# Linear attention and a routed expert layer on one core: the expert stage ordered without the rule that kept VectorE's two-operand instructions apart from GpSimd's gathers and scatters

## The chip, the cores and the metric

The kernel runs on one core of a Trainium2 chip. The metric is the device time of one execution in microseconds; lower is better. All times are of that one core.

## The reference

Two layers in a row. The first is a linear attention over 8 batches, 8 heads, 576 positions and 64 channels: queries and keys are projected to 128 features, shifted by their largest absolute value, and taken through exp(x) and exp(-x); the rows of the result, 4608 tokens of 512 numbers, go to the second layer. That is a layer of 8 experts with capacity: every token goes to one expert, every expert takes 576 tokens, and the pairs of token and expert are given out in the order of their logits.

```python
logits = x @ w_gate                       # 4608 x 8
order = np.argsort(-logits.flatten())
for idx in order:                         # greedy, cap = 576 tokens an expert
    tok, e = (int(idx) // E, int(idx) % E)
    if assigned[tok] >= 0 or counts[e] >= cap:
        continue
    assigned[tok] = e
    counts[e] += 1
for e in range(E):
    mask = assigned == e
    h = np.maximum(x[mask] @ w1[e], 0.0)  # 512 -> 1024
    out[mask] = h @ w2[e]                 # 1024 -> 512
```

## The kernel before, in words

The attention comes first (to about 310 us of the profile) and writes the token rows `xs` to HBM and the logits `L` to SBUF. The change does not touch it.

The greedy assignment is done expert by expert: of the experts still open, the one that fills first at the highest threshold gives up its 576 tokens, those are taken out of `L`, and the next is looked for. I number the experts 0 to 7 in the order in which they run. The routing of one expert (`routing`, lines 512 to 660) is a long chain of small steps between VectorE and TensorE: the key of each token's best logit is cut into six digits, and for each digit VectorE compares (L532), TensorE counts (L542 or L546), VectorE folds (L548, L550), TensorE sums (L553), VectorE makes a flag (L558), TensorE spreads it (L560), and VectorE picks the digit and goes on (L562, L566). Then ranks and indices are made (L584 to L648; the last matmul of that is L642, the index tile is `idx`), and the taken tokens are masked (L652 to L660, the step called `up`). The routing of expert r + 1 runs in the shadow of expert r's matmuls. Only expert 0's routing stands alone.

One expert's work: GpSimd gathers its 576 rows of `xs` with five indirect DMAs into `xg` (L751, the steps `ga`). TensorE transposes them in three sets (the steps `xp`: two sets of 16 matmuls at L771, one of 4 at L757; expert 0 has five sets of 4 at L757), ScalarE copies each into the rounded part `xh` (L758, L776), VectorE makes the remainder `xl` (L759, L777). The weights come through SP's queue as `raww` (L673), ScalarE rounds them (L735), VectorE makes the remainders `w1l` and `w2l` (L738, L739). The first layer is 16 products of 12 matmuls each (L797: rounded times rounded, and the two cross terms; 8 column blocks times two token halves of 272 and 304), each followed by a ReLU on ScalarE (L808, L809: `fh`, `ff`) and its remainder on VectorE (L812: `fl`). The second layer has five token blocks: four of 24 matmuls (L826, the steps `y`, planned in pairs) and one of 32 small ones (L841). ScalarE copies a block out of PSUM (L849, `ysb`), and GpSimd scatters it to the output with an indirect DMA (L855, the steps `ys`), after a small memset (L854).

What sets the order of all this is a planner, the class `Plan` (lines 18 to 90). Every step is put in with `add`: an engine, a planned duration, a due time, the steps it depends on, buffers it takes and frees, and a flag `lock`. `order` places them one after the other, always the step that can start earliest on its engine by the planned times, due times deciding. The result is fixed when the kernel is built: each engine's instructions stand in the order of the planned start times, and on the chip each engine takes them in that order and waits on semaphores for what isn't ready. The planned times themselves do nothing on the chip.

The flag `lock` has two sides in `order`, both for the plan alone (`self.dl` is the planned end of the last locked step of VectorE):

```python
if x['lock'] and e=='DVE': s=max(s,free.get('POOL',0.))
if x['lock'] and e=='POOL': s=max(s,self.dl)
```

A locked step of VectorE is planned to start when GpSimd is free; a locked step of GpSimd when the last locked step of VectorE has ended. In the expert stage the routing steps, the weight remainders, the gathers and the scatters have it.

Buffers that matter: one `xg`, one pair `xh`/`xl`, three `idx`, four PSUM buffers `h` shared by first-layer products and transposes, two `y`, two `ysb`.

## Time and profile before

| what | value |
|---|---|
| three runs | 808.28, 808.34 and 811.11 us, median 808.34 |
| the profiled execution | 810.09 us |
| its span, first to last instruction | 808.3 us |
| mean granted clock of TensorE | 0.975 |
| busy: TensorE | 770.2 us, 95% |
| busy: VectorE | 549.5 us, 68% |
| busy: ScalarE | 360.0 us, 45% |
| busy: GpSimd | 262.4 us, 32% |
| HBM read, written | 71.40 MB, 18.87 MB |

A row of the profile's groups reads: line, engine, operation, output<-inputs, shape, count | busy us, mean ns of one | idle time of the engine just before them, and what ended it. A row of the timeline reads: start us, length us, engine, line, operation, count [idle before <- what ended it]. PEld is TensorE's weight load, which overlaps its matmuls.

### The profile page before, as it was taken

To read this page: it belongs to the slowest core of one execution; us is meant where nothing else is said; L and a number is where in the kernel's file an instruction comes from. 1 tells how busy PE (TensorE), PEld (TensorE's weight loads), DVE (VectorE), ACT (ScalarE), POOL (GpSimd) and SP (SyncE) were. 2 spreads that over 40 slices of the span, in tenths; PEclk is the share of its full clock that TensorE was granted. 3 is DMA by queue.
4 is the path that set the end of the run, shared out by engine and by line. 5 is a ranking of instruction groups with operands and counts; after the bars stand their busy time and mean duration, and the time that the engine had idled before them with its cause. 6 is when DMAs were issued, how large, how long until landed. Compare 5 with 4: busy or idle time off the path is not lost.

```text
span 808.3 us, 23640 instructions
## 1 busy us (share of the span) xinstructions
PE 770.2 (95%) x10047; PEld 663.4 (82%) x10047; DVE 549.5 (68%) x1494; ACT 360.0 (45%) x625; POOL 262.4 (32%) x299
## 2 busy tenths in 40 slices
PE   6899999999999995599999999999999999999995
PEld 4788888888888885498798798798797897897983
DVE  5877888788788866787597486686585585550410
ACT  2866777676767750233343243233243233441410
POOL 3865555566665550300401302203103104302011
PEclk9999999999999996589999999999999999999998
DMA  8844454454444111532424415405323333801300
GB/s 181 178 120 120 135 147 135 127 150 134 128 120 119 33 37 56 163 105 82 158 88 133 130 66 157 155 18 187 137 63 128 137 100 116 273 2 41 124 27 32
DMA packets 73516, 91.80 MB, mean 114 GB/s; under 512 B 5155, under 2 KB 56515, under 8 KB 73411
## 3 DMA queue, kind: packets, MB, share of 16 engines
q1 hardware_dynamic: 67040, 71.06, 29.8%
q0 software_dynamic: 5952, 18.91, 7.1%
q8 instruction: 79, 1.29, 0.7%
q10 hardware_dynamic: 418, 0.33, 0.2%
q14 instruction: 27, 0.21, 0.1%
HBM read 71.40 MB, written 18.87 MB: 112 GB/s over the span
## 4 chain that ended last, share of the span: by engine, by line
PE 44%; issue 12%; POOL 2%; DVE 1%; DMA 0%; POOLq 0%; ACT 0%; DVEq 0%
PE h L797 20%; PE y L826 17%; PE y L841 2%; PE rps L546 1%; POOL out_dram L855 1%; PE rps L542 1%; PE h L771 1%; POOL xg L751 1%; PE h L757 1%; DMA xg<-xs,idx 0%; PE rps L623 0%; PE rps L560 0%; DVE cmp L618 0%; DVE cc L566 0%; POOLq L919 0%
## 5 line engine op out<-in xcount | busy, mean ns | idle before, releaser
L797 PE MATMUL h<-xh,w1h 128*128 128x272 f32 (+1 forms) x512 | 146.6, 307 | 0.7 <-ACT xh L758 0.7
L797 PE MATMUL h<-xh,w1l 128*128 128x272 f32 (+1 forms) x512 | 143.1, 299 | 0.0
L855 POOL DMA_INDIRECT out_dram<-ysb,idx x40 | 41.4, 1035 | 210.7 <-ACT ysb L849 201.0
L808 ACT ACTIVATE fh<-h 128x272 fp32r<-128x272 f32 (+1 forms) x128 | 49.3, 385 | 132.4 <-PE h L797 111.8
L826 PE MATMUL y<-w2h,fl 128*128 128x512 f32 x256 | 101.7, 397 | 0.0
L826 PE MATMUL y<-w2l,fh 128*128 128x512 f32 x256 | 101.1, 395 | 0.0
L826 PE MATMUL y<-w2h,fh 128*128 128x512 f32 x256 | 101.0, 394 | 0.0
L797 PEld LDWEIGHTS h<-xh,w1h 128*128 128x128 f32 x512 | 97.3, 190 | 2.0 <-ACT xh L758 1.1
L797 PEld LDWEIGHTS h<-xh,w1l 128*128 128x128 f32 x512 | 97.6, 191 | 0.0
L751 POOL DMA_INDIRECT xg<-xs,idx x40 | 40.5, 1012 | 172.6 <-issue 135.7
L797 PE MATMUL h<-xl,w1h 128*128 128x272 f32 (+1 forms) x512 | 91.4, 297 | 0.0
L270 ACT ACTIVATE qP<-D 128x768 f32<-128x768 f32 x96 | 72.8, 814 | 40.8 <-PE D L132 40.7
L812 DVE SCALAR_TENSOR_TENSOR fl<-h,fh 128x272 fp32r<-128x272 f32 (+1 forms) x128 | 52.6, 419 | 53.4 <-ACT fh L808 41.2
L211 POOL TENSOR_TENSOR ks<-ks,kP 128x512 f32<-128x512 f32 x64 | 81.6, 1278 | 4.6
L287 PE MATMUL D<-kz,qP 128*64 128x73 f32 x2304 | 79.9, 227 | 0.0
L287 PEld LDWEIGHTS D<-kz,qP 128*64 128x64 f32 x2304 | 75.4, 136 | 2.3
L210 POOL TENSOR_TENSOR ks<-kP 128x512 f32<-128x512 f32 x32 | 40.7, 1272 | 111.3 <-issue 87.2
L849 ACT COPY ysb<-y 128x512 f32<-128x512 f32 (+1 forms) x40 | 21.8, 545 | 122.4 <-PE y L826 58.8
L797 PEld LDWEIGHTS h<-xl,w1h 128*128 128x128 f32 x512 | 75.5, 188 | 0.0
L164 DVE TENSOR_REDUCE km<-D 128x6 f32<-128x768 f32 x48 | 45.7, 954 | 27.3 <-PE D L160 26.8
L198 PE MATMUL D<-kP,vi 128*64 128x256 f32 x512 | 61.8, 382 | 0.4 <-ACT kh L174 0.4
L164 DVE TENSOR_REDUCE qm<-D 128x6 f32<-128x768 f32 x48 | 45.5, 952 | 17.3 <-PE D L160 17.2
(179 smaller groups left out, 1461.7 us busy)
## 6 DMA issues: line engine op xcount, KB each, us to landing
raww<-in_moe_w_dram SPq DMA_DIRECT2D x64, 512.0 KB, 5.3
qi<-in_q_dram SPq DMA_DIRECT2D x32, 288.0 KB, 5.0
xs<-xp SPq DMA_DIRECT2D x16, 576.0 KB, 4.5
ki<-in_k_dram SPq DMA_DIRECT2D x32, 160.0 KB, 4.1
vi<-in_v_dram SPq DMA_DIRECT2D x32, 160.0 KB, 3.1
vi<-in_v_dram SPq DMA_DIRECT2D x32, 128.0 KB, 3.1
ki<-in_k_dram SPq DMA_DIRECT2D x30, 128.0 KB, 3.7
xg<-xs,idx POOLq DMA_INDIRECT x40, 3.5
```

The lines of the kernel that those rows point to most:

```text
L164: V.tensor_reduce(m[:,:,0:n],X['v'],axis=AX.X,op=OP.max,apply_absolute_value=True)
L198: PE.matmul(kv[64*c:64*c+64,i,0:256],v_[:,a,s_,:],kP[:,b,:],start=b in (0,5,9,14),stop=False,skip_group_check=True)
L210: if i==0: G.tensor_add(ks[:,:,a],X(0),X(1))
L211: elif i<3: G.tensor_add(ks[:,:,a],ks[:,:,a],X(i+1))
L270: for fh in range(2): A.activation(rows(qP[:,fh]),halves(X['T'],6),AF.Exp,scale=1.0-2*fh)
L287: PE.matmul(p[64*ab:64*ab+64,c,m:m+73],T['qP',u,jj][:,fh,o,64*ab:64*ab+64],T['kz',u][:,ab,fh,a^ab,:],start=fh==0,stop=fh==1,skip_group_che ...
L751: G.indirect_dma_start(out=T['xg',r][0:n,bb,:],out_offset=None,in_=xs,in_offset=bass.IndirectOffsetOnAxis(ap=T['idx',r][0:n,bb,:],axis=0))
L797: PE.matmul(p,ws[:,k,o:o+128],xx[:,k,o1:o2],start=n==0,stop=n==11)
L808: A.activation(hh[:,f,o1:o1+m1],p[:,0:m1],AF.Relu)
L812: V.scalar_tensor_tensor(hl[:,f,o1:o1+m1],p[:,0:m1],0.0,hh[:,f,o1:o1+m1],op0=OP.max,op1=OP.subtract)
L826: PE.matmul(p,hx[:,f,o:o+128],ws[:,f%2,:],start=n==0,stop=n==23)
L855: st=G.indirect_dma_start(out=ov,out_offset=bass.IndirectOffsetOnAxis(ap=iv,axis=0),in_=yv,in_offset=None)
```

## The change

Four lines of `moe` change. The flag `lock` goes from three steps: `up` of expert 0 on VectorE, every gather and every scatter on GpSimd. In the plan, GpSimd's gathers and scatters then no longer wait for VectorE's locked steps. VectorE's other locked steps (routing, weight remainders) keep the flag, and so still wait for GpSimd in the plan. The planned time of expert 0's transposes goes from 109 to 90 ns each. The long lines are the calls of `add` themselves.

```diff
--- before.py
+++ after.py
@@ -696,7 +696,7 @@
         return z
     def up0(x):
         for _ in it0: pass
-    add(('up',0),'DVE',1750.,2.,up0,lock=True)
+    add(('up',0),'DVE',1750.,2.,up0)
     prev=('up',0)
     for r in range(1,E):
         it=routing(r)
@@ -749,7 +749,7 @@
             def ga(y,r=r,bb=bb,n=n):
                 if bb==0: T['xg',r]=fp.tile([128,5,Dm],F32,name='xg',bufs=1)
                 G.indirect_dma_start(out=T['xg',r][0:n,bb,:],out_offset=None,in_=xs,in_offset=bass.IndirectOffsetOnAxis(ap=T['idx',r][0:n,bb,:],axis=0))
-            add(('ga',r,bb),'POOL',1250.,b+d['g']+.1*bb if r else bb*.1,ga,[('idx',r)] if r else [],slot=(('xg',1,('xg',r)),) if bb==0 else (),frees=(('idx',r),) if r else (),lat=2600.,lock=True,seq=('ga',r,bb-1) if bb else None)
+            add(('ga',r,bb),'POOL',1250.,b+d['g']+.1*bb if r else bb*.1,ga,[('idx',r)] if r else [],slot=(('xg',1,('xg',r)),) if bb==0 else (),frees=(('idx',r),) if r else (),lat=2600.,seq=('ga',r,bb-1) if bb else None)
             if r and bb<4: continue
             def xp_(y,r=r,bb=bb,o=o,n=n):
                 if bb==0: tokens(r)
@@ -758,7 +758,7 @@
             def xhf(y,r=r,bb=bb,o=o,n=n): A.copy(T['xt',r][0][:,:,o:o+n],T['xp',r,bb][:,:,0:n])
             def xlf(y,r=r,bb=bb,o=o,n=n): V.tensor_sub(T['xt',r][1][:,:,o:o+n],T['xp',r,bb][:,:,0:n],T['xt',r][0][:,:,o:o+n])
             due=b-d['TE']+d['xt']+2.8 if r else bb*.5
-            add(('xp',r,bb),'PE',4*(109. if n==128 else 62.),due,xp_,[('ga',r,bb)],seq=('xp',r,bb-1 if r==0 else 2) if bb else None,mode='A' if n==128 else 'H',slot=(('h',4,('xp',r,bb)),)+((('xt',1,('xt',r)),) if bb==0 else ()),frees=(('xg',r),))
+            add(('xp',r,bb),'PE',4*(90. if n==128 else 62.),due,xp_,[('ga',r,bb)],seq=('xp',r,bb-1 if r==0 else 2) if bb else None,mode='A' if n==128 else 'H',slot=(('h',4,('xp',r,bb)),)+((('xt',1,('xt',r)),) if bb==0 else ()),frees=(('xg',r),))
             add(('xh',r,bb),'ACT',70+.83*4*n,due+.5,xhf,[('xp',r,bb)])
             add(('xl',r,bb),'DVE',DV(4*n),due+1.,xlf,[('xh',r,bb)],frees=(('xp',r,bb),))
         for bb in (0,2) if r else ():
@@ -857,7 +857,7 @@
                 SC.append(st)
             due+=5.5 if nn==128 else 3.5
             add(('yc',r,bb),'ACT',480. if nn==128 else 280.,due+d['y'],yc,[lastq],slot=(('ysb',2,('ysb',r,bb)),),frees=(('y',r,bb),))
-            add(('ys',r,bb),'POOL',1250.,due+d['y']+.5,ys,[('yc',r,bb)],frees=(('ysb',r,bb),)+((('idx',r),) if r else ()),lat=2800.,lock=True)
+            add(('ys',r,bb),'POOL',1250.,due+d['y']+.5,ys,[('yc',r,bb)],frees=(('ysb',r,bb),)+((('idx',r),) if r else ()),lat=2800.)
     for i in range(cfg.get('warm',0)):
         if i%16==0: p=ps.tile([128,512],F32,name='h%d'%(i//16),bufs=1)
         PE.matmul(p[:,0:128],ones,ones,start=True,stop=True)
```

The program has the same instructions; what moves is their order, on every engine. Three places follow.

GpSimd, the gathers for expert 2 (tile `xg_7742` before, `xg_7725` now) among the scatters of expert 1's blocks (`ysb`). Before:

```order
L751 DMA xg_7742<-xs_57,idx_7708 128x512
L854 MEMSET spacer_776 1x1
L855 DMA out_0_dram<-ysb_7738,idx_6933 4608x512
L751 DMA xg_7742<-xs_57,idx_7708 128x512
L854 MEMSET spacer_776 1x1
L855 DMA out_0_dram<-ysb_7789,idx_6933 4608x512
L751 DMA xg_7742<-xs_57,idx_7708 128x512 x2
L854 MEMSET spacer_776 1x1
L855 DMA out_0_dram<-ysb_7862,idx_6933 4608x512
L751 DMA xg_7742<-xs_57,idx_7708 64x512
```

Now:

```order
L751 DMA xg_7725<-xs_57,idx_7696 128x512 x3
L854 MEMSET spacer_776 1x1
L855 DMA out_0_dram<-ysb_7753,idx_6933 4608x512
L751 DMA xg_7725<-xs_57,idx_7696 128x512
L751 DMA xg_7725<-xs_57,idx_7696 64x512
```

Before, scatters of three blocks stood between the five gathers; now one does. For experts 3, 4, 5 and 6 none does.

TensorE, the first transposes for expert 4 in expert 3's second layer; `y_9341` before is the PSUM tile of that layer's block 1, `y_9312` now that of its block 0. Before, the first set stands behind the whole of block 1:

```order
L826 MATMUL y_9341<-w2l_8972,fh 128x512
L826 MATMUL y_9341<-w2h_8971,fh 128x512
L826 MATMUL y_9341<-w2h_8971,fl 128x512
L826 MATMUL y_9341<-w2l_8972,fh 128x512
L771 MATMUL h_9390<-ident,xg 128x64
```

Now it stands behind the 14th matmul of block 0:

```order
L826 MATMUL y_9312<-w2h_8968,fl 128x512
L826 MATMUL y_9312<-w2l_8969,fh 128x512
L826 MATMUL y_9312<-w2h_8994,fh 128x512
L826 MATMUL y_9312<-w2h_8994,fl 128x512
L771 MATMUL h_9353<-ident,xg 128x64
```

The transposes come 34 second-layer matmuls earlier in the stream, and the routing of expert 5 that follows them moves ahead with them. So it is, by 10 to 34 matmuls, for experts 1 to 6.

TensorE, the start of the expert stage, expert 0's transposes (L757) and first products (L797). Before:

```order
L757 MATMUL h_6309<-ident,xg 128x128 x4
L797 MATMUL h_6320<-xh,w1h_6261 128x272
L797 MATMUL h_6320<-xh,w1l_6262 128x272
L797 MATMUL h_6320<-xh,w1h_6261 128x272
L757 MATMUL h_6334<-ident,xg 128x128 x4
```

Now:

```order
L757 MATMUL h_6309<-ident,xg 128x128 x4
L757 MATMUL h_6320<-ident,xg 128x128 x4
L797 MATMUL h_6325<-xh,w1h_6261 128x272
L797 MATMUL h_6325<-xh,w1l_6262 128x272
L797 MATMUL h_6325<-xh,w1h_6261 128x272
```

The fourth set of transposes has changed places with three matmuls. On ScalarE, the second of the token copies (L758) now stands ahead of the weight cast (L735) that stood ahead of it.

## The prediction

> **What bounds the kernel now.** I read first the page's slices of time, then the stretches of single experts, then who waited for whom, then the chain that ended last. The slices put the TensorE row beside its granted clock:
>
> ```profile
> PE   6899999999999995599999999999999999999995
> ...
> PEclk9999999999999996589999999999999999999998
> ```
>
> There are two holes only: the routing of expert 0 (slices 16 and 17, about 310 to 340 us, where the clock falls as well), and the end. I call the experts 0 to 7 in the order in which they run. The expert stage is everything behind the hole. In the table of stretches (length, then busy us and count of PE, PEld, DVE, ACT, POOL, then granted clock) one expert's period reads
>
> ```profile
> 404.00:462.00 58.00, 58.00 (x465) 50.46 (x466) 42.17 (x134) 20.40 (x43) 10.59 (x15) 1.00 0.33 104
> ```
>
> TensorE is busy 58.00 of 58.00 us at full clock, VectorE 42.17 and GpSimd 10.59. A busy TensorE is modelled, so I look at who waited between 404 and 809 us. Asked for TensorE's matmuls alone the list is empty; GpSimd's gathers are the ones that sit still, and nothing that the profile shows ends it:
>
> ```profile
> POOL xg L751 <- issue: 130.5, 29, 32.0
> ```
>
> The groups by form show the idle time ahead of the matmuls in the last column, and it is zero:
>
> ```profile
> L826 PE MATMUL y<-w2h,fl 128*128 128x512 f32 x224 | 89.1, 398 | 0.0
> L797 PE MATMUL h<-xh,w1h 128*128 128x304 f32 x224 | 66.2, 311 | 0.0
> ```
>
> The chain that ended last gives the true spacing of the stream (start, length, what, count):
>
> ```profile
> 438.71 11.00 PE y L826 x48
> 449.71 0.65 PE h L771 x16
> 450.36 4.77 PE y L826 x20
> ...
> 487.97 3.27 PE h L797 x24
> ```
>
> That is 0.229 us a second-layer matmul, 0.458 for the pair that the planner moves as one step, 0.136 us a first-layer matmul, 0.65 for a set of 16 transposes, and no gap between them. The stage is a packed matmul stream. Edits of order can't take matmuls out of it; they can only open waits in it, or shorten the hole ahead of it. A measurement of this kernel can tell about 0.5% (4 us) from no change.
>
> **The change part by part.** No instruction is added or removed. Three locks and one planned duration go from the planner, so it no longer holds a gather or a scatter back until VectorE's planned two-operand work ends, and no longer holds back the step that ends expert 0's routing. VectorE's own locked steps still wait, in the plan, for GpSimd. The outcome is an order.
>
> *The start.* Expert 0's fourth set of transposes now stands ahead of the first three matmuls; on ScalarE the second token copy stands ahead of a weight cast that used to precede it. The rows of this place, from the timeline, the tile xg (time to landing, between 320 and 350 us) and the stretches:
>
> ```profile
> 338.89 0.95 POOL L751 DMA_INDIRECT xg<-xs,idx  x1 [0.30 <-issue]
> 339.69 1.05 ACT L735 CAST w1h<-raww 128x1024 fp32r<-128x1024 f32 x1
> 341.27 0.59 ACT L758 CAST xh<-h 128x512 fp32r<-128x512 f32 x1 [0.53 <-PE h L757]
> 343.00 0.60 PE L797 MATMUL h<-xh,w1h 128*128 128x272 f32 x1 [0.68 <-ACT xh L758]
> 343.84 1.06 PE L757 MATMUL h<-ident,xg 128*128 128x128 f32 x4
> 344.55 0.58 PE L797 MATMUL h<-xh,w1l 128*128 128x272 f32 x1
> ...
> DMA to landing us min/median/max: 3.2/3.8/4.5
> ...
> 344.00:346.00 2.00, 2.00 (x11) 2.00 (x10) 2.00 (x6) 0.59 (x1) 0.00 (x0) 0.50 0.04 8
> 346.00:348.00 2.00, 2.00 (x19) 1.73 (x18) 1.97 (x6) 0.14 (x1) 0.00 (x0) 0.50 0.00 0
> ```
>
> The fourth gather lands at 338.89 + 3.8 = 342.7, while TensorE is idle, so its transposes fill a hole instead of taking 344.55 - 343.84 = 0.7 us of the stream. But the third copy now comes behind the cast: 341.27 + 0.59 + 1.05 + 0.59 = 343.5 instead of 343.0, so 0.5 to 0.6 is given back. Net about -0.2 us. The bounds: 0, if a step of expert 1's routing ends last here anyway; and -2.2, if the fuller stream also brought the full clock back at 344 instead of past 348 (4 us at 0.50 are worth 2 us). I take -0.2, since what TensorE does between 342 and 345 hardly gets denser.
>
> *Gathers against transposes, experts 1 to 4.* Before, the transposes of the next expert's tokens stood late in the second layer. Now the planner believes the gathers to be back to back and puts them as early as it thinks the rows arrive: the first set for expert 2 moves from the end of block 2 to the middle of block 1. Whether the rows are there is to be worked out from the step that makes the indices (the matmul of L642). Expert 2 in the trace:
>
> ```profile
> 438.53 0.18 PE L642 MATMUL rps<-d,dup 128*128 128x18 bf16 x1
> ...
> 440.08 1.13 POOL L751 DMA_INDIRECT xg<-xs,idx  x1 [34.47 <-PE y L826]
> 441.21 0.09 POOL L854 MEMSET spacer<- 1x1 f32 x1
> 441.51 0.99 POOL L855 DMA_INDIRECT out_dram<-ysb,idx  x1 [0.21 <-ACT w1h L735]
> ...
> 447.41 0.98 POOL L751 DMA_INDIRECT xg<-xs,idx  x1 [0.30 <-issue]
> 448.70 0.96 POOL L751 DMA_INDIRECT xg<-xs,idx  x1 [0.30 <-issue]
> ...
> DMA to landing us min/median/max: 2.8/3.4/3.6
> ```
>
> The first gather starts 1.55 us behind L642, the second 1.13 + 0.30 = 1.43 later, each further one 1.28 (0.98 + 0.30), and a landing takes 3.4. Now three gathers stand ahead of the first scatter. The second lands at 1.55 + 1.43 + 3.4 = 6.4; TensorE gets to the first set behind 15 pairs, at 15 x 0.458 = 6.9: no wait, 0.5 to spare (before: 449.7 against a landing by about 446). The fourth gather waits for a scatter, which waits for a block that ends at 8 pairs = 3.7 and its copy: scatter at about 5.5, fourth gather at 6.8, landed at 10.2; TensorE is there at 6.9 + 0.65 + 6 x 0.458 = 10.3. The fifth lands at 6.8 + 1.28 + 3.4 = 11.5, TensorE comes at 10.3 + 0.65 + 0.46 = 11.4. So expert 2 waits 0.1 us, or 0.5 if a copy comes late. Expert 4 is the tightest:
>
> ```profile
> 551.53 0.18 PE L642 MATMUL rps<-d,dup 128*128 128x18 bf16 x1
> ...
> 553.59 1.12 POOL L751 DMA_INDIRECT xg<-xs,idx  x1 [31.24 <-issue]
> ```
>
> Its gathers start 2.06 behind L642; all five now go in a row, the fourth at 2.06 + 1.43 + 2 x 1.28 = 6.05, landed at 9.45. TensorE has 30 first-layer matmuls (4.1), 7 pairs (3.2), a set (0.65) and 3 pairs (1.4) ahead of the second set: 9.35. That is 0.1 late, the fifth gather another 0.1; one more relu remainder ahead of the index step on VectorE may add 0.4 to each: 0.2 to 0.9, and I take 0.3. Expert 3 has the same form and I give it 0.2; expert 1, whose routing order is unchanged and which keeps about 0.5 to spare, gets none. Experts 5 to 7 gather long before, their transposes being held by the token buffer. Sum +0.6, bounds 0 and 3 x 0.9 = 2.7.
>
> *Routing of expert 7 inside expert 5.* There VectorE now has, between the index comparison and the step that TensorE's L642 waits for, two relu remainders, two weight remainders and the masking pair, and then the token remainder that frees the buffer for the last transposes:
>
> ```profile
> L812 DVE SCALAR_TENSOR_TENSOR fl<-h,fh 128x272 fp32r<-128x272 f32 x56 | 24.4, 436 | 40.3 <-ACT fh L808 40.2
> L738 DVE TENSOR_TENSOR w1l<-raww,w1h 128x512 fp32r<-128x512 f32 x53 | 35.3, 684 | 1.2 <-ACT w1h L735 1.1
> L637 DVE TENSOR_TENSOR pm<-rps,msk 128x36 f32<-128x36 f32 x6 | 1.2, 197 | 6.0 <-PE rps L623 6.0
> ```
>
> 2 x 0.44 + 2 x 0.68 + 2 x 0.20 = 2.6 us. TensorE in the same time has the 18 counting matmuls (0.46), a set (0.65) and a pair (0.46) = 1.6. If it reached the count just as the comparison ends it would wait 1.0; if VectorE is a microsecond ahead, nothing. I take +0.4.
>
> The sum: -0.2 + 0.6 + 0.4 = +0.8 us. The profiled execution took 810.09 us, its span 808.3 and 1.8 around it, so it would take 810.9. The median of the runs shown, 808.34, is 1.75 below the profiled one; the forecast for it is 808.34 + 0.8 = 809.1 us.
>
> **The rivals.** *No new waits at all.* The planned gather is longer than the measured one, so everything may be there in time; then only the start counts: -0.2, at most -2.2, thus 806.1 to 808.1. For it speaks that no row of before names a wait of TensorE, although its order was made by the same greedy rule.
>
> *Gathers held by VectorE, with no rule to keep them apart* (slower). The longest gather of before ran under a chain of weight remainders:
>
> ```profile
> 689.12 2.48 DVE L738 TENSOR_TENSOR w1l<-raww,w1h 128x512 fp32r<-128x512 f32 x4
> ...
> 690.96 1.49 POOL L751 DMA_INDIRECT xg<-xs,idx  x1 [0.30 <-issue]
> ...
> L751 POOL DMA_INDIRECT xg<-xs,idx x10: 903/970/1485, 668.1 to 698.2; - x10
> ```
>
> 1.49 against a median of 0.97 is 0.5 us. Were each of five gathers held so, the last would come 2.5 late, and experts 2, 3 and 4, which have no reserve, would wait 2.5 each, expert 1 2.0: +9.5, so 818. It decides from about 0.2 us a gather on. Against it: in before, gathers overlapped such work in plenty (440.08 took 1.13), since the lock held in the plan alone. The Trainium skill, "SBUF — State Buffer", section "Who interferes with whom", has this rival as a rule: a VectorE instruction with two SBUF inputs contends with a GpSimd instruction that reads SBUF, and whichever comes second is blocked for the whole of the first. By that rule the removed locks were worth up to a weight remainder per gather; the 1.49 agrees with some holding, the median does not agree with a full one.
>
> *The routing chain gets tight* (slower). A digit's step on VectorE in the second layer, with one weight remainder between, is
>
> ```profile
> L562 DVE TENSOR_REDUCE ch<-rps 128x1 f32<-128x8 f32 x30 | 5.0, 165 | 11.4 <-PE rps L560 10.9
> L566 DVE SCALAR_TENSOR_TENSOR cc<-cc,ch,dg 128x36 bf16<-128x36 bf16 x20 | 5.1, 256 | 0.7
> L532 DVE TENSOR_TENSOR cmp<-cc,kt 128x1152 bf16<-128x1152 bf16 x35 | 25.5, 753 | 0.3
> ```
>
> 0.17 + 0.26 + 0.68 + 0.75 = 1.9 us and about 0.2 for the product's end, against 5 pairs = 2.3 us. One more weight remainder late and TensorE waits 0.3; at three digits of five experts that is +4.5, and 813.
>
> **How the numbers follow.** Forecast (few short waits) 0.60, no new waits 0.25, gathers held 0.06, tight chain 0.09. Faster by over 0.5% needs 4 us out of a stream without gaps: 0.02, from the far end of the clock bound. Slower: the two last rivals but for their mild half, and the tail of the forecast's bounds: 0.12. The rest, 0.86, is the same. The range takes in the no-wait case down to -1.3 (it leaves out the last 0.9 of the clock bound), and upward the bounds 2.7 + 1.0 and one microsecond of the tight chain: 807.0 to 813.0.
>
> **What would show it.** Right: the same packed periods, TensorE's idle time in waits for xg no more than a microsecond in all, gathers of experts 2 to 4 in rows of three to five, transposes right behind their landing, ScalarE's third copy at 343.5. Wrong: transposes that wait over a microsecond for xg (gathers held if L751 grows past 1.1 us on average), waits of L546, L553 or L560 for VectorE (tight chain), or an expert period under 57 us, which nothing here explains.

## The result and the profile after

| | runs | median us | range us |
|---|---|---|---|
| before | 4 | 809.21 | 808.28 to 811.11 |
| after | 4 | 815.06 | 814.74 to 815.77 |

The ratio is 1.0063, 95% interval 1.0041 to 1.0084: slower by 0.6%, about 5 us, where 809.1 (807.0 to 813.0) was forecast. The profiled execution took 815.13 us, its span 813.4, against 810.09 and 808.3 before.

The slices of time of the changed kernel, TensorE and its granted clock, look like those of before:

```profile
PE   6999999999999995599999999999999999999995
...
PEclk8999999999999996699999999999999999999998
```

The last matmul of the kernel ends at 799.0 us before and 804.1 after. To keep the start out of it I measure the full stream from its 49th first-layer matmul (353.2 us before, 352.3 after) to its last matmul: there the changed kernel is 5.9 us longer. So the loss arises inside the stream, and the profiled execution had gained 0.8 at its start. The stretches of the changed kernel (length, busy us and count of PE, PEld, DVE, ACT, POOL, clock, DMA share, GB/s) show where the packed stream has holes: the first period has 1.5 us without a busy TensorE, a later one 0.1.

```profile
404.00:462.00 58.00, 57.88 (x464) 49.25 (x462) 42.31 (x134) 19.38 (x42) 10.28 (x15) 1.00 0.34 114
348.00:406.00 58.00, 56.48 (x454) 47.72 (x455) 43.28 (x138) 19.55 (x41) 9.46 (x13) 1.00 0.34 110
```

Asked for TensorE's waits between 348 and 809 us, before has none. After has these (waited for; us in total, times, longest):

```profile
PE rps L546 <- DVE cmp L532: 2.0, 2, 1.4
PE h L771 <- DMA xg<-xs,idx: 0.6, 2, 0.3
```

The wait for rows is the 0.6 us that the forecast had. The first line is new: L546 is the count of the first digit of the next expert's routing, and it waits for VectorE's comparison. The list names 2.6 us. Measured from start to start, the larger gaps in the matmul stream are 1.57 us at 397.1 (L546), 0.85 at 501 (rows), 0.75 at 616 (L546), 0.28 twice (L553), 0.20 (L546) and 0.17 (L642). Together they are 4.1 of the 5.9 us; the rest isn't broken down here.

Why is the comparison late? Before, the first set of transposes for expert 1, and ScalarE's copies of it, stand so in the timeline:

```profile
393.66 0.71 PE L771 MATMUL h<-ident,xg 64*128 64x64 f32 x16
394.41 1.07 ACT L776 CAST xh<-h 128x512 fp32r<-128x512 f32 x2 [0.92 <-PE h L771]
```

The first copy starts 0.04 us behind the set's end at 394.37. In the changed kernel the set runs 3.1 us earlier, and the copies hardly move:

```profile
390.57 0.71 PE L771 MATMUL h<-ident,xg 64*128 64x64 f32 x16
393.77 1.08 ACT L776 CAST xh<-h 128x512 fp32r<-128x512 f32 x2 [5.64 <-PE y L826]
394.39 0.69 DVE L777 TENSOR_TENSOR xl<-h,xh 128x512 fp32r<-128x512 f32 x1 [5.93 <-ACT xh L776]
...
397.14 0.68 DVE L738 TENSOR_TENSOR w1l<-raww,w1h 128x512 fp32r<-128x512 f32 x1
397.74 0.44 DVE L471 TENSOR_TENSOR OH<-scb,sm 128x288 bf16<-128x288 bf16 x1
398.11 0.74 DVE L532 TENSOR_TENSOR cmp<-dg,kt 128x1152 bf16<-128x1152 bf16 x1
...
398.91 0.39 PE L546 MATMUL rps<-OH,cmp 128*128 128x32 bf16 x9 [1.41 <-DVE cmp L532]
```

The set ends at 391.28. ScalarE has been idle for 5.64 us and starts at 393.77, 2.5 us late; VectorE has been idle for 5.93. The timeline names a matmul of L826 as what released ScalarE, but the copy reads L771's tile: what came late is TensorE's report that the set was done. The trace's semaphore events agree: TensorE's count for the set goes up at 393.69. Before, of 408 such reports between 345 and 809 us none is over 0.2 us late; their median is 0.014. In the changed kernel 23 of 415 are. From the late copy on the chain is plain: the token remainders (L777) stand ahead of the masks and the comparison in VectorE's queue, the comparison ends 1.4 us after TensorE wants it, and TensorE stands still.

### The profile page after: what moved, and what is told of

The parts are those of the page before. It is cut to its first block, busy times and chain, and to the rows that moved or that the text cites. A ratio compares the mean times of both kernels' runs of the same rounds, so it can differ in the third digit from the quotient of the medians.

```text
span 813.4 us, 23643 instructions
## 1 busy us (share of the span) xinstructions
PE 772.0 (95%) x10047; PEld 660.7 (81%) x10047; DVE 548.1 (67%) x1494; ACT 358.1 (44%) x625; POOL 262.7 (32%) x299
## 3 DMA queue, kind: packets, MB, share of 16 engines
q8 instruction: 79, 1.29, 0.7%
## 4 chain that ended last, share of the span: by engine, by line
PE 40%; issue 14%; DVE 4%; POOL 3%; DMA 1%; ACT 0%; POOLq 0%; DVEq 0%; ACTq 0%
PE h L797 19%; PE y L826 13%; PE y L841 2%; POOL out_dram L855 2%; PE rps L546 1%; PE rps L542 1%; POOL xg L751 1%; DVE xl L777 1%; PE h L771 1%; DMA xg<-xs,idx 1%; PE h L863 1%; DVE cmp L532 0%; PE rps L623 0%; PE h L757 0%; DVE w1l L738 0%
## 5 line engine op out<-in xcount | busy, mean ns | idle before, releaser
L797 PE MATMUL h<-xh,w1h 128*128 128x272 f32 (+1 forms) x512 | 143.9, 303 | 0.3 <-ACT xh L758 0.3
L797 PE MATMUL h<-xh,w1l 128*128 128x272 f32 (+1 forms) x512 | 141.3, 297 | 0.0
L826 PE MATMUL y<-w2l,fh 128*128 128x512 f32 x256 | 102.3, 400 | 0.0
L826 PE MATMUL y<-w2h,fh 128*128 128x512 f32 x256 | 102.1, 399 | 0.0
L826 PE MATMUL y<-w2h,fl 128*128 128x512 f32 x256 | 102.1, 399 | 0.0
L797 PEld LDWEIGHTS h<-xh,w1h 128*128 128x128 f32 x512 | 96.6, 189 | 2.1 <-issue 1.2
L797 PEld LDWEIGHTS h<-xh,w1l 128*128 128x128 f32 x512 | 96.7, 189 | 0.2
L797 PE MATMUL h<-xl,w1h 128*128 128x272 f32 (+1 forms) x512 | 91.7, 297 | 0.0
L751 POOL DMA_INDIRECT xg<-xs,idx x40 | 40.4, 1010 | 144.5 <-PE h L797 68.8
L797 PEld LDWEIGHTS h<-xl,w1h 128*128 128x128 f32 x512 | 75.4, 188 | 0.0
```

The lines of the kernel that those rows point to most:

```text
L751: G.indirect_dma_start(out=T['xg',r][0:n,bb,:],out_offset=None,in_=xs,in_offset=bass.IndirectOffsetOnAxis(ap=T['idx',r][0:n,bb,:],axis=0))
L797: PE.matmul(p,ws[:,k,o:o+128],xx[:,k,o1:o2],start=n==0,stop=n==11)
L826: PE.matmul(p,hx[:,f,o:o+128],ws[:,f%2,:],start=n==0,stop=n==23)
```

## The experiments

One table for all runs of whole kernels. The third column is the time from the end of the first set to its first copy, for the transposes of experts 1 to 6. Then comes what TensorE waits between 348 and 809 us for L532 (at L546) and for rows (at L771) in the profiled execution, and how much longer than before the stream of that execution is, measured as above. The last column is the ratio to the kernel before, with its interval.

| kernel | us | first copies late, us | L546 | rows | stream | ratio |
|---|---|---|---|---|---|---|
| before | | 0.04, 0.08, 0.03, 0.03, 0.03, 0.03 | 0 | 0 | 0 | 1 |
| after | 815.06 | 2.49, 2.46, 1.41, 1.31, 0.24, 0.23 | 2.0 | 0.6 | 5.88 | 1.0063 (1.0041 to 1.0084) |
| 1 second set later | 812.64 | 2.41, 1.66, 1.07, 1.43, 0.95, 0.98 | 1.7 | 0 | 2.95 | 1.0039 (1.0026 to 1.0052) |
| 2 all sets later | 811.22 | 1.13, 0.04, 0.04, 0.04, 0.04, 0.04 | 0.6 | 0 | 1.39 | 1.0035 (1.0021 to 1.0049) |
| 3 gathers' lock alone | 814.64 | 2.34, 0.93, 1.09, 1.37, 1.22, 1.01 | 1.5 | 1.2 | 4.67 | 1.0071 (1.0054 to 1.0088) |
| 4 scatters' lock alone | 808.68 | 0.04, 0.37, 0.04, 0.59, 0.59, 0.52 | 0 | 0 | -0.66 | 0.9993 (0.9984 to 1.0002) |
| 5 remainders behind | 814.52 | 0.43, 0.38, 1.43, 0.60, 0.45, 1.14 | 0 | 2.6 | 6.26 | 1.0048 (1.0029 to 1.0067) |
| 6 locks kept, sets early | 810.46 | 0.37, 0.07, 0.67, 0.66, 0.68, 0.03 | 0 | 0 | -0.20 | 0.9995 (0.9981 to 1.0009) |
| 7 longer VectorE plan | 813.57 | 2.08, 2.51, 1.88, 1.71, 0.90, 1.12 | 2.0 | 0 | 4.25 | 1.0042 (1.0027 to 1.0057) |
| 8 start alone | 809.59 | 0.04, 0.09, 0.03, 0.03, 0.03, 0.03 | 0 | 0 | 0.00 | 0.9996 (0.9981 to 1.0010) |
| 9 all sets far | 809.32 | 0.04, 0.04, 0.03, 0.03, 0.04, 0.04 | 0 | 0 | -0.31 | 0.9984 (0.9969 to 0.9999) |
| 10 third gather held | 807.59 | 0.09, 0.03, 0.03, 0.03, 0.03, 0.03 | 0 | 0 | -1.01 | 0.9977 (0.9966 to 0.9989) |
| 11 its order, no hold | 810.15 | 2.40, 0.25, 1.05, 0.25, 1.30, 1.25 | 1.1 | 0 | 0.23 | 1.0004 (0.9993 to 1.0016) |
| 12 hold, short landings | 810.09 | 0.51, 0.50, 0.15, 0.42, 0.15, 0.62 | 0 | 0 | 0.35 | 0.9998 (0.9985 to 1.0010) |
| 13 its order, no hold | 810.09 | 0.09, 0.04, 0.04, 0.03, 0.03, 0.04 | 0 | 0 | 0.32 | 1.0003 (0.9991 to 1.0014) |
| 14 changed order, hold | 813.88 | 0.09, 0.03, 0.04, 0.03, 0.24, 0.23 | 0 | 2.5 | 4.65 | 1.0045 (1.0030 to 1.0060) |
| 15 changed kernel again | 816.16 | 2.49, 2.43, 1.39, 1.29, 0.23, 0.23 | 2.2 | 0.4 | 5.74 | 1.0077 (1.0056 to 1.0099) |

The 0.24 and 0.23 of experts 5 and 6 in the changed kernel are ScalarE's own: TensorE's report comes within 0.01 us there.

The first theory was that TensorE's queue, which runs ahead of what it executes, sits in the second set's wait for its gather, and that reports of finished work stay behind until it gets past. In the changed kernel the first set's report came within 0.05 us of an event of the fourth gather at each of experts 1 to 4, 3.30 to 3.38 us behind that gather's start. Rivals: the early first set as such; VectorE's planned durations; the scatters; the start.

**1 and 2: where the sets stand.** From the changed kernel, one number each.

```diff
-...lat=2600.,seq=('ga',r,bb-1)...
+...lat=2600. if bb<2 else 5200.,seq=...     (1)
+...lat=5200.,seq=...                        (2)
```

> The changed kernel with one number more: the plan counts 5200 instead of 2600 ns from a gather to its rows for the third, fourth and fifth gather of an expert (the first two keep 2600). So the first set of transposes keeps its early place (6.9 us of TensorE work behind the index matmul L642) and the second set moves back, from 2.0 to 3.9 us of TensorE work behind the first to 4.8 to 6.1 us. Late-report theory (the first set's completion is reported only when TensorE's queue, which has already come to the second set, gets past its wait for the gather; the copies, the token remainders on VectorE and the first digit's comparison slip, and L546 waits): the reports come within 0.1 us of the set's end, L546's waits between 340 and 809 us fall from 2.9 to under 0.8 us, time 809 to 811. Rival, the first set as such is too early (its copies and token remainders stand ahead of the routing on VectorE, so the routing is late whatever TensorE reports): L546's waits stay at 2 to 3 us, time 813 to 816. Rival, VectorE's planned durations are too short for an order without slack: no change, 814 to 816.

> The changed kernel with 5200 instead of 2600 ns planned from every gather to its rows: both sets move back by about 2.7 us (first set at 9.6 us behind L642, second 2.5 to 3.4 us behind the first), while the gathers go as early as in the changed kernel. Late-report theory: the rows of the fourth gather are there (by about 9.5 to 10.2 us behind L642) before or just when TensorE's queue comes to the second set, some 3.3 us before it executes it, so the report is late by 0.6 us at most; time 809 to 811. VectorE durations too short: 813 to 816, since VectorE's load and its planned slack are those of the changed kernel. Gathers that lie under VectorE's two-operand work cost time by themselves: also 813 to 816, since the gathers stay where they are.

In run 1 the second set stood 4.2 to 5.6 us behind the first one, its rows long there when it ran, and the first copies were late all the same. So the place of the second set doesn't explain it: the first form of the theory fell. A tie to the fourth gather itself is not refuted by this run, since the reports come 3.1 to 3.3 us behind its start at five of the six experts here too. Run 2 has prompt reports from expert 2 on, and the L546 wait of expert 1's place alone. By the ratios it gives back nearly half, and in the profiled stream 4.5 of the 5.9 us, although three of its gathers took 2.42 us (more of that below).

**3, 4 and 8: which edit.** The kernel before, with one lock off each, or with the two edits of the start.

```diff
-add(('ga',r,bb),'POOL',1250.,...,lat=2600.,lock=True,seq=...)
+add(('ga',r,bb),'POOL',1250.,...,lat=2600.,seq=...)          (3)
-add(('ys',r,bb),'POOL',1250.,...,lat=2800.,lock=True)
+add(('ys',r,bb),'POOL',1250.,...,lat=2800.)                  (4)
-add(('up',0),'DVE',1750.,2.,up0,lock=True)
+add(('up',0),'DVE',1750.,2.,up0)                             (8)
-add(('xp',r,bb),'PE',4*(109. if ...
+add(('xp',r,bb),'PE',4*(90. if ...                           (8)
```

> The kernel before with the lock taken from the gathers alone (scatters, the end of expert 0's routing and the 109 ns stay). First set at 6.9 us behind L642, second 2.5 to 3.9 us behind the first, gathers in rows of three to five. Late-report theory: reports late by 1.3 to 2.5 us at experts 1 to 4 as in the changed kernel, L546 waits 2 to 3 us, time 812 to 816. If the loss comes from scatters that go earlier or from the start: 808 to 810.

> The kernel before with the lock taken from the scatters alone. The gathers stay split by scatters, first set at 8.7 to 9.2 us behind L642, second 4.3 to 7.0 us behind it. Late-report theory: the queue comes to the second set about 3.3 us before it executes, so later than the first set's end; the report is prompt or late by under 0.5 us; time 808.5 to 811. If the scatters (or ScalarE's copies for them) carry the loss: 812 to 816.

> The kernel before with only the two edits that act at the start: no lock on the step that ends expert 0's routing, 90 instead of 109 ns for a transpose of a full block. The experts keep their order. All theories: within 1 us of the kernel before (the forecast gave this part -0.2 us, bounds 0 and -2.2). Were the missing 5 us in the start, this kernel would show them.

The gathers' lock carries the whole loss; scatters and start carry nothing that can be measured. Run 8's profiled execution also shows how far the start varies by itself: it lay 3.18 us behind before's at expert 0's last block and by the same 3.18 at every later expert. Its granted clock was 0.50 until 353.7 us, against 348.4 before.

**5 and 7: VectorE's order and its plan.** From the changed kernel.

```diff
-add(('xl',r,bb+i),...,[('xh',r,bb+i)],...)
+add(('xl',r,bb+i),...,[('xh',r,bb+i)]+([('rt',r+1,5)] if bb==0 and r<E-2 else []),...)   (5)
-DV=lambda n: 55.+1.03*n
+DV=lambda n: 155.+1.03*n                                                                 (7)
```

> The changed kernel, with the two token remainders of the first set put behind the first digit's comparison of the next routing on VectorE (one more dependency in the plan). Sets and gathers keep their early places. If the late report costs only because those remainders stand ahead of the comparison on VectorE: reports stay late by 0.9 to 2.4 us, but L546 no longer waits for the comparison (under 0.5 us in all), time 808.5 to 811. If TensorE or the gathers lose time in another way: 813 to 816.

> The changed kernel with 100 ns more planned for each weight, token and relu remainder on VectorE, so that the planned 682 ns meet the measured 684. Sets stay close behind their rows (first set at 6.9 to 8.2 us behind L642). If the planner's short VectorE durations are the cause: L546 and L553 stop waiting, 808 to 810.5. Late-report theory: reports late by 1 to 2 us at most experts, time 811 to 815.

Run 5 did what was asked of it: no wait of L546. But the time stayed, with another wait in its place (the waits of TensorE between 348 and 809 us):

```profile
PE h L771 <- DMA xg<-xs,idx: 2.6, 4, 1.4
```

So this order has two tight deadlines, the first count and the later sets' rows; with one loosened, the other shows. My expectation of 808.5 to 811 was wrong by that. The edit moved other work as well, so it doesn't show that the one wait alone brought the other. Run 7 clears VectorE's planned durations of the charge: the waits of L546 stayed.

**6, and a plain stream.** Second form of the theory: a set that runs within about 2 us of its rows' landing is reported late. Run 6 is the kernel before with every lock and `lat=600.` for the gathers. A kernel of its own measured the report in a plain stream of second-layer matmuls.

> The kernel before, every lock kept, with 600 instead of 2600 ns planned from a gather to its rows: the gathers stay split by scatters, and the first set of an expert moves ahead by 1.8 to 2.3 us of TensorE work (to 6.9, at expert 2 8.7 us behind L642), the second set follows 5.2 us behind it. Second form of the late-report theory: 0.2 to 1.1 us between landing and set, reports late by 1 to 2.3 us, time 811 to 814 although no lock is gone. First form: prompt, since the second set is far behind, 808 to 810. If the place of the gathers beside VectorE's two-operand work is what costs: 808 to 810.

> A kernel that leaves out the whole computation (it writes zeros) and measures one thing. TensorE runs an unbroken stream of second-layer matmuls (128x512); in it stand sets of eight 64x64 transposes whose rows come by a gather, each set copied by ScalarE. Fourteen cases: no gather at all; a set that follows the landing of its rows by about 4, 3, 2, 1.5, 0.8 and 0.2 us; four cases with a second set whose gather lands while the first set is queued or done (the first set about 0.8 or 4 us behind its rows); and three cases in which the set waits for VectorE instead of a gather, by 0 to 1.6 us. Read: from the end of a set to the start of its copy. First form of the theory (the wait of the second set for its gather holds the first set's report back): prompt (under 0.1 us) in all cases with one set, late by 1 to 2.5 us in the cases with two. Second form, to which the runs before point (a set is reported late if TensorE's queue has only just come past the wait for the set's own rows): prompt from about 2.2 us between landing and set, late by 0.9 to 2.4 us below that, with or without a second set. If it is the transfer and not the wait, the cases with VectorE are prompt; if it is any wait that leaves the queue empty, they are late as well.

> Again a kernel that leaves out the whole computation and writes zeros. The first one never had a set closer than 1.25 us behind its rows, and every report in it was prompt. Now as in the expert stage: two gathers for a set, sixteen 64x64 transposes, ScalarE copies. 24 cases: two gathers alone, with the set 0 to 2 us behind the second landing; the same with three more gathers in flight behind them; the same with a second set that waits for the third and fourth gather, 17 or 30 matmuls behind the first; and a set that waits for VectorE by 0 to 1 us. Theory, any close wait leaves TensorE's queue empty and holds reports back while it fills: late by 0.5 to 2 us below about 1 us of slack in all four groups. Theory, later gathers in flight hold the report back: prompt in the first and the last group, late in the second and third. Theory, the second set's wait: late in the third group alone. If all are prompt, the delay needs something of the expert stage that this kernel lacks, and stays unexplained.

In run 6 the first sets started some 0.4 to 1.25 us behind the landing of their rows, as close as in the changed kernel; copies were late by 0.7 us at most, and nothing was lost. In the plain stream all 48 sets of both kernels were copied 0.03 to 0.09 us behind their end. One of the closest, whose second gather had landed at 58.02:

```profile
58.24 0.71 PE L59 MATMUL A<-ident,x 64*128 64x64 f32 x16
59.05 1.07 ACT L63 CAST sA<-A 128x512 fp32r<-128x512 f32 x2 [31.73 <-PE A L59]
```

Nearness alone is not enough either. The late report needs something of the expert stage that a plain stream lacks.

**9: enough distance.** The changed kernel with `lat=5800.` for every gather.

> The changed kernel with 5800 ns planned from every gather to its rows (2600 in the changed kernel, 5200 in the run before that moved all sets back): first set at 10.1 to 10.5 us of TensorE work behind L642, second 2.0 to 3.4 us behind it, so every set 2.5 us or more behind its rows. If the nearness of sets and rows is the whole loss: no report late by over 0.5 us, no wait of L546 over 0.5 us, 808.5 to 810.5. If gathers without a lock cost something of their own: 811 to 813.

```profile
393.91 0.72 PE L771 MATMUL h<-ident,xg 64*128 64x64 f32 x16
394.67 1.07 ACT L776 CAST xh<-h 128x512 fp32r<-128x512 f32 x2 [1.37 <-PE h L771]
```

The three locks are off as in the changed kernel, every report is prompt, and the loss is gone, with a trace of gain. And this although the gathers meet more of VectorE's work than in the changed kernel. A gather took 1156 ns on average instead of 1010, and the fifth one for expert 4 took 2.42 us, under three instructions in a row that read two operands each:

```profile
553.37 2.42 POOL L751 DMA_INDIRECT xg<-xs,idx  x1 [0.31 <-issue]
...
553.30 0.68 DVE L738 TENSOR_TENSOR w1l<-raww,w1h 128x512 fp32r<-128x512 f32 x1
553.90 0.44 DVE L471 TENSOR_TENSOR OH<-scb,sm 128x288 bf16<-128x288 bf16 x1
554.27 0.74 DVE L532 TENSOR_TENSOR cmp<-dg,kt 128x1152 bf16<-128x1152 bf16 x1
```

VectorE's three end at 555.01, the gather 0.78 us later. Runs 2, 5 and 9 have ten gathers of 2.09 us or more under these three, all ending 0.78 to 0.85 us behind them. So what the lock was meant to prevent does happen without it; in the changed kernel no gather met all three, and its longest took 1.47. Run 9 says that neither this nor the missing lock costs time once every set has distance in the plan.

**10 to 14: a gather in flight.** Third form: it is the next gather, issued while the first set runs. In run 10 GpSimd clears the rows of blocks 2 to 4 ahead of the third gather, which holds it back; run 11 has the same order without the clearing. The clearing is a line more in the kernel, so in runs 10, 12 and 14 L771 reads L772, and L776 reads L777.

```diff
 def ga(y,r=r,bb=bb,n=n):
     if bb==0: T['xg',r]=fp.tile([128,5,Dm],F32,name='xg',bufs=1)
+    if r and bb==2: G.memset(T['xg',r][:,2:5,:],0.0)             (10, 12, 14)
-add(('ga',r,bb),'POOL',1250.,...,lat=2600.,...)
+add(('ga',r,bb),'POOL',3000. if r and bb==2 else 1250.,...)      (10 to 13)
+...lat=2600. if bb<2 else 5200.,...                              (10, 11)
```

> The kernel of the first experiment (second set planned later, first set close behind its rows), in which GpSimd also clears the rows of blocks 2 to 4 ahead of an expert's third gather, so that this gather starts some 2 us later and no further gather is in flight when the first set runs. The output is the same, since the gathers write these rows afterwards. Theory, later gathers in flight hold the report back: late by 0.65 us at most, as in the run with the locks kept, time 808.5 to 811. Theory, nearness of set and rows as such: late by 0.9 to 2.3 us as in the first experiment, time 811.5 to 813.5.

> The kernel of the held third gather without the clearing that holds it: the same order of the work on every engine, the plan still counts 3000 ns on GpSimd for the third gather, but the chip issues it right behind the instruction ahead of it, some 1.4 us earlier. Theory, a gather in flight when the first set runs holds the report back: late by 0.9 to 2.4 us again, time 810.5 to 813. Theory, the order alone (the second set far behind the first) is what helped: reports prompt, 806.5 to 808.5.

Run 10, GpSimd, TensorE and ScalarE around the first set of expert 1:

```profile
388.51 1.40 POOL L751 MEMSET xg<- 128x1536 f32 x1
390.19 0.97 POOL L752 DMA_INDIRECT xg<-xs,idx  x1 [0.27 <-POOL xg L751]
...
390.32 0.71 PE L772 MATMUL h<-ident,xg 64*128 64x64 f32 x16
...
391.12 1.08 ACT L777 CAST xh<-h 128x512 fp32r<-128x512 f32 x2 [3.24 <-PE h L772]
```

Run 11, the same three:

```profile
389.94 0.97 POOL L751 DMA_INDIRECT xg<-xs,idx  x1 [0.31 <-issue]
...
391.44 0.71 PE L771 MATMUL h<-ident,xg 64*128 64x64 f32 x16
...
394.55 1.07 ACT L776 CAST xh<-h 128x512 fp32r<-128x512 f32 x2 [5.55 <-PE y L826]
```

In the same order the hold takes the third gather from 1.5 us ahead of the set to 0.13, the copy from 2.40 us late to 0.09, and the ratio from 1.0004 to 0.9977. Run 10 beats the kernel before by 1.4 us at the medians of their comparison (807.59 against 808.97). Run 11 fits neither expectation: its copies are late at four experts and L546 waits 1.1 us, yet it is level with the kernel before. Two more kernels and a second plain stream then went against the theory:

> The changed kernel with the hold alone: clearing ahead of the third gather and 3000 ns planned for it, every landing planned at 2600 ns as in the changed kernel. First set close behind its rows, second set 3.9 to 5.2 us behind the first, by estimate 0.5 to 2 us behind its rows. In-flight theory: the first set's reports are prompt (under 0.2 us), the second set's may be late by up to 0.6; L546 waits under 1 us; 807.5 to 810. Nearness theory: 811 to 815.

> The kernel of the run with the hold and short planned landings, without the clearing: the same order (second set 3.9 to 5.2 us behind the first), the third gather issued right behind the instruction ahead of it. In-flight theory: the first set's copies start 0.9 to 2.4 us late at most experts, L546 waits for VectorE again, 811 to 814, so 1.5 to 4 us above the run with the hold. If the order alone brought the time back: 809 to 810.5.

> The changed kernel, its plan and order untouched, with the clearing ahead of an expert's third gather. The gathers come 1.4 us later, so by the order of the changed kernel the second set (2.0 to 3.9 us behind the first) now finds its rows missing: by estimate 0.3 to 1.5 us at each of experts 1 to 6, TensorE waiting for xg 2 to 6 us in all, while the first set's reports come within 0.6 us and L546 stops waiting. 811 to 815. If the early third gather were harmless, L546 would wait as in the changed kernel and the rows on top: 816 to 820.

> The plain stream again (no part of the reference is computed, zeros are written), five gathers a case, the first set 0 to 1.2 us behind its rows, with what the stream lacked: weight loads in flight (8 of 512 KB), VectorE two-operand work, a further matmul that waits for VectorE eight matmuls behind the first set, and all of these together; a second set waits for its gathers in three cases of four. Read: from a set's end to its copy's start. The factor that holds the report back shows late by 0.5 to 2.4 us in its group and in the group with all; if all stay prompt, it is none of these.

Run 13 has no hold, its third gather starts 1.5 us ahead of the set as in runs 1 and 11, and the copy follows the set's end (390.93) at once:

```profile
388.71 0.97 POOL L751 DMA_INDIRECT xg<-xs,idx  x1 [0.31 <-issue]
...
390.22 0.71 PE L771 MATMUL h<-ident,xg 64*128 64x64 f32 x16
...
391.03 1.07 ACT L776 CAST xh<-h 128x512 fp32r<-128x512 f32 x2 [3.24 <-PE h L771]
```

So a gather in flight isn't enough either, and the last plain stream, with five gathers, weight loads, VectorE work and a further wait, had prompt copies throughout (35 sets, 0.03 to 0.09 us). Run 14 is the changed order with the hold alone. The first sets' copies are prompt at experts 1 to 4, L546 no longer waits, and the rows take over, as expected from a clearing that itself makes the gathers 1.4 us later:

```profile
PE h L772 <- DMA xg<-xs,idx: 2.5, 4, 1.0
```

Runs 12 and 13 keep the landings at 2600 ns and plan 1750 ns more for the third gather alone. At experts 1 to 4 that puts the second set 4.3 to 5.2 us of TensorE work behind the first instead of 2.0 to 3.9, and it was enough to be level with the kernel before, hold or no hold.

**15: once more.**

> The changed kernel once more, nothing edited. If the late report belongs to its order: the first set's copies start 1.3 to 2.5 us behind the sets of experts 1 to 4 again, L546 waits 2 us or more in all between 348 and 809 us, ratio 1.005 to 1.008. If the late report belongs to a single execution and carries the loss: prompt copies, no wait of L546, and a profiled time near 810. If prompt copies come with 814 to 816 all the same, the late report is a sign and not the cause.

The delays came back within 0.03 us at all six experts, and the waits with them:

```profile
PE rps L546 <- DVE cmp L532: 2.2, 3, 1.4
PE h L771 <- DMA xg<-xs,idx: 0.4, 1, 0.4
```

The late report belongs to the changed kernel as a program, not to one execution. So does the loss in the stream: 5.74 us here, 5.88 in the first execution.

**A mark that goes with the late reports.** A gather or scatter counts up its semaphore in 16 steps, and the trace has an event for each: 1280 for a kernel's 80 in the expert stage. Before, and in runs 8, 9, 10, 13 and 14, all 1280 are there. In the changed kernel 902 are, and in the other runs 830 to 1023; the first of the missing ones are those of expert 0's gathers, at 337 us. The list of transfers shows it, before and after, by the median time to landing, which it can't give for the changed kernel:

```profile
xg<-xs,idx POOLq DMA_INDIRECT x40, 3.5
...
xg<-xs,idx POOLq DMA_INDIRECT x40
```

Between 345 and 809 us no kernel with all events has a report of TensorE over 0.2 us late; each of the others has 17 to 27, the level runs 4, 6, 11 and 12 among them. The plain streams lack three events or none, and all their reports are prompt. Runs 1 and 13 put it most plainly. At experts 1, 2 and 4 their first sets stand alike to 0.05 us against the second, third and fourth gather, and the copies are 2.41, 1.66 and 1.43 us late in run 1, and 0.09, 0.04 and 0.03 in run 13. What puts a program on one side or the other isn't shown; run 15 came out on the changed kernel's side again.

For the experiments this means that runs 9, 10, 13 and 14 differ from the changed kernel in their order and in this mark, so what they gain can't be put down to the order alone. The mark by itself costs nothing: runs 4, 6, 11 and 12 carry it and are level. In one order the kernel that carries it has 1.2 us more of stream (11 against 10), in another there is no difference (12 against 13). Of the kernels that lose time all carry it but run 14, whose gathers the clearing delays.

**What is settled and what isn't.** Shown: the loss comes with the gathers' lock (3; not 4, 8). It goes when the plan puts the sets, or the third gather and what stands behind it, far enough back, with the lock still off (9, 11, 12, 13); 11 and 12 have late reports all the same. Run 1 moves the second sets alone and gets only half of the stream back. The wait that is visible in the changed kernel comes from copies that start up to 2.49 us late; where that wait is gone in a tight order (5, 14), the later sets wait for rows, in 14 with the clearing's own delay. Not settled: what holds a finished set's report back. The second set's place (1), nearness (6, 10, 13), a gather in flight (13) and a single execution (15) are each not enough alone; the missing events go with it in every run. Nor is there a run of the changed order with prompt reports and undelayed gathers, so how much of its loss would remain then is open. Of the 2.1 us that run 10's profiled execution is ahead of before's, 1.1 lie at the start, which varies; where the 1.0 in the stream comes from isn't shown.

## Why the prediction was wrong, step by step

- **What bounds the kernel: right.** TensorE's stream is the bound, and what lengthens it are waits in it. That order can't take time out of the stream held but for 0.7 us in run 4 and 1.0 in run 10.
- **The start, -0.2 us: smaller than its own spread.** The first matmul of the first layer starts at 343.01 against 343.00. From 353 us on the profiled changed kernel is 0.8 us ahead; its granted clock was 1.00 from 343.8 us, against 348.4 before, as the far bound had it, but TensorE waited for part of that stretch. The same program lay 1.6 us behind in run 15 and the same start 3.2 behind in run 8, and run 8's ratio shows no difference that can be measured.
- **Gathers against transposes, experts 1 to 4, +0.6 us with 2.7 at most: the step that failed.** Its own quantity came out as forecast: TensorE waits 0.6 us for rows. But the step asked only whether TensorE waits, not who else does: it moved the first set 3 us ahead and took for granted that the copies and the token remainders move with it, where the remainders stand in VectorE's queue ahead of the next first count. The copies came 2.5 us late, and 1.57 us of TensorE's time went at expert 1's place alone; at L546 and L553 it lost 3.1 us in all, and 0.85 for rows. The bound of 2.7 was no bound, because it had rows as the only thing that could be late. The late report could not be read from the trace of before, where the first sets ran 1.35 us (expert 6) to 3.5 us behind their rows and every report was prompt; that the remainders stand ahead of the comparison, could. About 1.8 of the 5.9 us remain without a named gap.
- **Routing of expert 7 inside expert 5, +0.4 us: right in place, half in size.** The gap there, at L642, is 0.17 us.
- **Gathers held by VectorE, chance 0.06: not in this kernel, but real.** The groups by form, all gathers of each kernel, after, before and in run 9:

```profile
L751 POOL DMA_INDIRECT xg<-xs,idx x40 | 40.4, 1010 | 144.5 <-PE h L797 68.8 <-issue 63.0 <-PE y L826 10.1
```

```profile
L751 POOL DMA_INDIRECT xg<-xs,idx x40 | 40.5, 1012 | 172.6 <-issue 135.7 <-PE y L826 34.5 <-DVE idx L632 2.5
```

```profile
L751 POOL DMA_INDIRECT xg<-xs,idx x40 | 46.2, 1156 | 152.2 <-issue 96.3 <-PE h L797 48.1 <-DVE idx L648 5.4
```

  1010 ns against 1012, with the lock off: in the changed kernel the gathers aren't held more than before. The average hides what each meets, though. Before, the 11 gathers that overlap a weight remainder took 1.15 us, the other 29 took 0.96, which a median over all of them can't show; after, it is 1.15 (9) and 0.97 (31). In run 9 the overlapping ones took 1.48 (14). The sign that the prediction set for this rival, over 1.1 us on average, is met there and in runs 2 and 5, and run 9 still loses nothing. The Trainium skill, "SBUF — State Buffer", section "Who interferes with whom", would have a GpSimd instruction that reads SBUF wait out a whole two-input VectorE instruction. Run 9's gather of 2.42 us, which ends 0.78 us behind such work, agrees with it.
- **The routing chain gets tight, chance 0.09, 813 us: the nearest.** It named the sign that came, L546 waiting for VectorE's comparison. Its mechanism was another: 15 digits late by 0.3 us each because of one more weight remainder. (By its own rows, 1.9 + 0.2 + 0.7 against 2.3, it should have said 0.5.) What came was the first digit alone, 1.4 us late at the worst, behind token remainders that waited for ScalarE.
- **No new waits, chance 0.25: wrong,** for the same reason as the failed step.

## What to carry to other kernels

A rule in a scheduler can be worth its time for a reason other than its own. This one guarded against gathers held by VectorE, which cost run 9 nothing; what it gave here was distance between a transfer and its consumers. When an edit lets a planner put work earlier, follow each moved step to everything queued behind it on the engines that come after it, and ask what a microsecond of lateness in any one of them would hold up, before calling the cover free. And when one wait is removed and the time stays, look for the next deadline in the same place, and give the plan distance there instead of tuning one edge.

## What the runs showed of the hardware

- A finished set of transposes can be reported to the other engines 0.9 to 2.5 us after its end (changed kernel at experts 1 to 4, most first sets of runs 1, 3, 7 and 11, and some of runs 2 and 5), with ScalarE idle all the while. A second execution of the same program repeats it to within 0.03 us. In the kernel before and in runs 8, 9, 10, 13 and 14, whose instructions are the same but for the clearing, it takes 0.01 to 0.03. The views show it as an idle time ahead of the copy, put down to a later matmul.
- In every kernel with reports over 0.2 us late the trace lacks 20% or more of the landing events of gathers and scatters (257 to 450 of 1280); in every kernel without them it has all. Which is cause and which is effect isn't shown.
- A clearing of 128x1536 on GpSimd (1.40 us), set ahead of the third gather, went with prompt reports in two pairs (run 10 against 11, run 14 against the changed kernel), but in a third the kernel with the clearing has the late copies (0.15 to 0.62 us in run 12, 0.09 at most in run 13). So it isn't what makes reports prompt.
- An indirect gather on GpSimd that starts under a chain of VectorE's two-operand instructions ends 0.78 to 0.85 us behind the chain: 2.1 to 2.4 us instead of 0.96 (runs 2, 5, 9).
